# A recurrent attention kernel on one core: working tiles share fewer buffers, a turned operand is kept in DRAM, and more of a streamed weight stays in SBUF

## The chip, the cores and the metric

The kernel runs on one core of a Trainium2 chip. The metric is the device time of one launch in microseconds. Before the change three runs took 2093.66, 2095.27 and 2100.72 us, median 2095.27. One further execution, taken with the hardware profiler, gave the page and the trace that are read below.

## The reference, cut to what matters

```python
x  = A_x                                   # [1, 2048, 1024] bf16
xn = layernorm(x)
out = x + A(xn, mem0, Wq, Wk, Wv, Wo) + B(xn, w_r, w_gate, w_up, w_down)

def A(x, mem0, ...):                       # 32 heads of 128, segments of 32 rows, M = 8 memory rows
    mem = mem0
    for s in range(64):
        h = concat(mem, x[32*s : 32*s+32])              # 40 rows
        q, k, v = h @ Wq, h @ Wk, h @ Wv                # 1024 x 4096 each
        p = softmax(mask(q @ k.T * 128**-0.5))          # memory rows see all; others causal
        o = (p @ v) @ Wo                                # 4096 x 1024
        mem = o[:8]                                     # recurrence
        outs.append(o[8:])

def B(x, ...):                             # router r = x @ w_r picks 2 of the 2048 rows; they alone get
    ...                                    # silu(x@w_gate) * (x@w_up) @ w_down * sigmoid(r), added to x
```

So 64 steps follow one another, each with only 40 rows against four weight matrices of 8 MB, and the memory rows of a step need the end of the step before.

## The kernel before, in words

**Rows.** The 8 memory rows and the first 24 rows of a segment make up the 32 "main" rows of a step (XM = 24, XL = 8). The last 8 rows of a segment, the "left" rows, don't depend on the recurrence until attention. They are gathered for four segments at a time: a group G is four steps, j = s % 4, and its 32 left rows go through Q, K, V as one operand STL in the steps before they are needed. `left_of(s)` says which matrix's left pass a step carries: V of its own group in j=0, Q of the next group in j=1, K of the next group in j=2, nothing in j=3.

**Weights.** The four matrices are cut into 64 granules of 128 x 2048 bf16 (512 KB): 48 for Q, K and V in six phases p0 to p5 of eight (`PHASES`: Q half 0, K half 0, Q half 1, K half 1, V half 0, V half 1), then 16 for Wo (w = 0 to 15, two heads each). 43 granules stay in SBUF for the whole kernel (`wres`). 21 are streamed again in every step from packed copies in DRAM (`wsc`) through a pool of five 4 KB slots (`g`), in order, by SP's queue; `after(s, g)` issues the load of the next streamed granule when one was used. Three streamed granules are partly kept elsewhere: granule 10 wholly and granule 19 by half in PSUM (KEPT, copied into the slot by ACT and DVE), and of granule 35 (HALF, the V phase) the first 1024 columns in the SBUF tile HB. So a step reads 18 granules of 512 KB and two halves of 256 KB.

**A step.** PE takes the granules in order: four column-tiled matmuls with ST (the turned main rows, L638), and where a left pass is due four more with STL (L621). Work that hangs between granules is hooked by (phase, granule): `hook(2, 6, scores(0))` runs after granule 6 of phase 2. After each of p0 to p3 ACT copies the result to XB (L654), PE turns it at (p+1, 3) and ACT or DVE copies it to QT or KT; after p4 and p5 ACT copies VM (L674), and in j=0 VL (L678). `scores` and `soften` run on PE, DVE and ACT, `attend` at (5,5), (5,7), w=5 and w=8. `add_x` at (5,3) starts WO in a PSUM buffer of the pool psA (two buffers, which PSm shares). The projection L689 takes the 16 Wo granules. Then ACT and DVE copy WO to OB, four POOL DMAs store the rows (L748), PE turns OB, and DVE writes the memory rows into the next ST (L281): the next step starts.

**Left rows.** In j=1 and j=2 the results of the left pass go by ACT to XBl (L659, in the single buffer "bD") and by four POOL DMAs to ql_d in DRAM (L664), at hook (p+1, 5); each step loads its part as LX (L454), which PE turns and ACT copies to QKL at (1,5). The left outputs of a group are accumulated in WL (PSUM, pool psL, one buffer "accl" shared with PSl and OPa): in j=3, streamed granules right behind WO's matmuls, the resident ones partly in `fill` at the step's end and five in the next step. x of the left rows comes in at w=1 by a matmul with IDENT on XL (L725), which `sum_left` has scaled on DVE at (5,6). In the next j=0, at (3,0), ACT copies WL to OL (buffer "vl", which VL uses from the end of p4) and POOL stores it (L762).

**STL.** In j=0 XL of the next group is loaded at (3,0), normed by DVE at (5,6), turned by PE at w=13 and copied by ACT to STL (L304 to L308); the first four left passes of the next step run already as `fill` at the end of j=0.

**The first step** (s=0) loads everything: all weights, x (`load_x`, 4 MB), and DRAM-to-DRAM copies of the streamed granules by POOL (`copy_block`). In it DVE takes the row statistics of the 16 x tiles after granules 1 to 15, and after granules 18 to 33 `router_tile(t)`: L223 writes the normed tile to XR, L225 multiplies it with w_r, sums it and writes its products over XR. The last ten resident granules live in the homes of x tiles, XR and MISC, so they are loaded late.

**Buffers.** The pool "one" has one buffer for each tag: bA, bB, bC, bD, bE of 1 KB, kt, st, stl, otl, vl and a few small ones. A new tile of a tag waits until the readers of the last one are done. PTB, the PSUM tile for all transposes, is a single buffer too. The order on each engine is the order of the program (manual schedule); POOL and SP issue their DMAs in order.

Of the kernel before, what the change touches and what calls it, by code (L numbers as in the profile page):

```python
# [8 lines left out]
BF16 = mybir.dt.bfloat16  # L9
F32 = mybir.dt.float32  # L10
# [18 lines left out]
def kernel(  # L29
# [102 lines left out]
    HB = const.tile([P, 1024], BF16, name="HB")  # L132
# [87 lines left out]

    def router_tile(t):
        XR = home(hx, [P, D], BF16, "XR")
        nc.vector.tensor_scalar(out=XR[:, :], in0=xt(t), scalar1=RI16[:, t, 0:1], scalar2=RI16[:, t, 1:2],  # L223
                                op0=ALU.subtract, op1=ALU.mult)
        nc.vector.tensor_tensor_reduce(out=XR[:, :], in0=XR[:, :], in1=WRB, scale=1.0, scalar=0.0,  # L225
                                       op0=ALU.mult, op1=ALU.add, accum_out=RF[:, t:t + 1])
# [91 lines left out]
    def fetch():  # L318
        if not flow:
            return  # L320
        s, g = flow.pop(0)
        t = wstream.tile([P, 2048], BF16, tag="g", name="g")
        c = columns(g, s)
        if s == 0 and g == HALF:
            nc.sync.dma_start(out=HB[:, :], in_=granule_dram(g)[:, 0:1024])
            nc.sync.dma_start(out=t[:, c], in_=granule_dram(g)[:, c])
        elif s == 0:
            nc.sync.dma_start(out=granule_out(t, g), in_=granule_dram(g))
        elif c is not None:
            nc.sync.dma_start(out=t[:, c], in_=wsc[g][:, :])  # L330
        queued.append((g, t))

    def part(g, t, jq):
        return HB[:, 512 * jq:512 * (jq + 1)] if g == HALF and jq < 2 else t[:, 512 * jq:512 * (jq + 1)]


    def keep(g, t):
        for c, K in KEPT_COLS[g].items():
# [4 lines left out]
            XK = one.tile([P, 512], BF16, tag="kt", name="XK")  # L343
# [145 lines left out]
    for s in range(NSEG):  # L489
# [9 lines left out]
        def transposes(mat, half, XB):  # L499
# [13 lines left out]
        def left_keys(half):  # L513
            nc.vector.tensor_copy(out=KT[half][:, :, 32:NK], in_=qkl[0][:, :, 2 * half + 1, :])  # L514
# [66 lines left out]
        def get_left():  # L581
            nxt["xl"] = load_left(G if j == 3 else G + 1)

        def prep_left():
            if j == 0:
                norm_left(nxt["xl"], G + 1)
            else:
                sum_left(nxt["xl"], G)

# [35 lines left out]
        for p, (mat, half) in enumerate(PHASES):  # L625
# [26 lines left out]
            if mat < 2:  # L652
                XB = one.tile([P, 512], BF16, tag=("bC", "bA")[half], name="XB")
# [3 lines left out]
                def store_ql(mat=mat, half=half, PSl=PSl):  # L657
                    XBl = one.tile([P, 512], BF16, tag="bA" if s == 0 and mat == 1 and half == 0 else "bD", name="XBl")
# [22 lines left out]
        WO = nxt["wo"]  # L681
        if s + 1 < NSEG:
            new_lx(s + 1)

        def project(PS, w, Gv, lhs, last):
            for hs in range(2):
                h = 2 * w + hs
                for g in range(4):
                    nc.tensor.matmul(PS[32 * g:32 * g + 32, 0:256], lhsT=lhs(h),  # L689
                                     rhs=Gv[:, D * hs + 256 * g:D * hs + 256 * (g + 1)], start=False,  # L690
# [15 lines left out]
        behind = []  # L706
        for w in range(16):
            if w == 5:
                attend(1, 0)
            if w == 8:  # L710
                attend(1, 1)
            Gv = granule(48 + w)
            project(WO, w, Gv, lhs_main, w == 15)
            if j == 3:
                if w in home_w:
# [3 lines left out]
                    else:  # L719
                        todo.append(((2, (1, 2, 4, 5, 7)[len(todo)]), fn))  # L720
                else:
                    behind.append((w, Gv))
                if w == 1:
                    WL = psL.tile([P, 512], F32, tag="accl", name="WL")
                    nc.tensor.matmul(WL[:, 0:256], lhsT=IDENT[:, :], rhs=nxt["xl"][:, :], start=True, stop=False,  # L725
                                     skip_group_check=True)
                if w >= 1:
                    for w_, Gv_ in behind:
                        project(WL, w_, Gv_, lhs_left, False)
                    behind = []  # L730
# [25 lines left out]
        if j == 3:  # L756
# [6 lines left out]
            todo.append(((3, 0), store_left))  # L763
# [107 lines left out]
```

## Time and profile before

| what | value |
|---|---|
| median of three timed runs | 2095.27 us |
| profiled execution, its own time | 2080.72 us |
| its span (first to last instruction) | 2079.2 us |
| mean granted TensorE clock | 0.948 |
| PE / weight loads / DVE / ACT / POOL busy | 80% / 43% / 41% / 32% / 29% |
| SP's hardware queue | 687.69 MB, 89.1% of 16 DMA engines' span |
| POOL's software queue | 36.34 MB, 5.5% |
| first step (to the first L281 after it) | ends at 132.2 us |
| 63 further steps | about 29.9 us each, to 1982.5 us |
| the rest (last step and the two expert rows) | to 2079.2 us |

A page gives for each group of instructions its line, engine, operation, the tiles it writes and reads, how many there are, their busy time and mean, and the idle time of that engine just before them with what ended it ("issue" is time in which the engine waited for nothing that the profile shows). [...]

### The profile page before, as it was taken

To read this page: it belongs to the slowest core of one execution; us is meant where nothing else is said; L and a number is where in the kernel's file an instruction comes from. 1 tells how busy PE (TensorE), PEld (TensorE's weight loads), DVE (VectorE), ACT (ScalarE), POOL (GpSimd) and SP (SyncE) were. 2 spreads that over 40 slices of the span, in tenths; PEclk is the share of its full clock that TensorE was granted. 3 is DMA by queue.
4 is the path that set the end of the run, shared out by engine and by line. 5 is a ranking of instruction groups with operands and counts; after the bars stand their busy time and mean duration, and the time that the engine had idled before them with its cause. 6 is when DMAs were issued, how large, how long until landed. Compare 5 with 4: busy or idle time off the path is not lost.

```text
span 2079.2 us, 82974 instructions
## 1 busy us (share of the span) xinstructions
PE 1671.3 (80%) x36024; PEld 893.3 (43%) x36024; DVE 846.3 (41%) x2716; ACT 670.8 (32%) x1867; POOL 597.2 (29%) x1142
## 2 busy tenths in 40 slices
PE   3568888888798888888888888888888788888855
PEld 1224444444354444445444444444444444544433
DVE  5733343444434433443444434433443344344420
ACT  0123333333333233333333333333333333333320
POOL 3313233323333232333323232332323223322120
PEclk8679999999999999999999999999999999999986
DMA  9999999999999899999999999999999999999996
GB/s 365 402 350 370 337 340 346 347 347 354 361 334 375 316 342 340 347 368 331 368 340 362 359 353 360 347 372 344 366 341 346 332 359 353 330 360 350 366 389 261
DMA packets 244925, 729.33 MB, mean 351 GB/s; under 512 B 49616, under 2 KB 55792, under 8 KB 244560
## 3 DMA queue, kind: packets, MB, share of 16 engines
q1 hardware_dynamic: 203584, 687.69, 89.1%
q0 software_dynamic: 40976, 36.34, 5.5%
q8 instruction: 282, 4.62, 0.9%
q14 instruction: 83, 0.68, 0.1%
HBM read 711.09 MB, written 22.55 MB: 353 GB/s over the span
## 4 chain that ended last, share of the span: by engine, by line
DMA 59%; PE 28%; issue 5%; ACT 4%; POOL 2%; DVE 1%; ACTq 0%; SPq 0%; POOLq 0%; DVEq 0%
DMA g<-wsc 45%; PE PSm L638 12%; PE WO L689 5%; PE PSl L621 3%; DMA out_dram<-OL 3%; DMA ql_d<-XBl 3%; PE WL L689 2%; DMA wres<-in_A_Wo_dram 2%; PE BT L502 1%; DMA XP<-in_A_x_dram 1%; POOL out_dram L762 1%; POOL ql_d L664 1%; DMA g<-in_A_Wv_dram 1%; DMA out_dram<-XN 1%; DMA wres<-in_A_Wq_dram 1%
## 5 line engine op out<-in xcount | busy, mean ns | idle before, releaser
L638 PE MATMUL PSm<-wres,ST 128*32 128x512 bf16 x8192 | 705.5, 388 | 7.8 <-DVE ST L281 5.4
L638 PEld LDWEIGHTS <-ST 128*32 128x32 bf16 x12288 | 324.3, 96 | 505.2 <-issue 229.6
L638 PE MATMUL PSm<-g,ST 128*32 128x512 bf16 x3968 | 414.9, 389 | 144.8 <-DMA g<-wsc 125.3
L654 ACT CAST XB<-PSm 128x512 bf16<-128x512 f32 x256 | 150.4, 587 | 413.6 <-PE PSm L638 409.9
L748 POOL DMA_DIRECT2D out_dram<-XN x256 | 131.2, 519 | 505.3 <-DVE XN L746 489.4
L689 PEld LDWEIGHTS <-OT 128*32 128x32 bf16 x8192 | 208.1, 99 | 122.5 <-issue 95.7
L689 PE MATMUL WO<-wres,OT 128*32 128x256 bf16 x5632 | 236.3, 283 | 15.9 <-DMA wres<-in_A_Wo_dram 13.6
L664 POOL DMA_DIRECT2D ql_d<-XBl x256 | 154.2, 609 | 297.6 <-ACT XBl L659 292.0
L621 PE MATMUL PSl<-wres,STL 128*32 128x512 bf16 x2048 | 195.4, 392 | 12.2 <-ACT VL L678 11.4
L689 PE MATMUL WO<-g,OT 128*32 128x256 bf16 x2560 | 135.7, 288 | 69.2 <-DMA g<-wsc 58.6
L251 POOL DMA_DIRECT2D XN<-in_A_x_dram x256 | 130.3, 512 | 126.6 <-PE BT L502 45.2
L454 POOL DMA_DIRECT2D LX<-ql_d x63 | 36.6, 581 | 403.3 <-ACT OT L573 220.5
L511 DVE COPY KT<-BT 128x512 bf16<-128x512 bf16 x128 | 54.4, 425 | 224.0 <-PE BT L502 224.0
L674 ACT CAST VM<-PSm 128x512 bf16<-128x512 f32 x128 | 77.7, 607 | 163.8 <-PE PSm L638 159.4
L350 DVE COPY g<-KEPT 128x512 bf16<-128x512 bf16 x252 | 95.1, 419 | 71.7 <-PE PSm L638 46.4
L502 PE MATMUL BT<-IDENT,XB 128*128 128x128 bf16 x1024 | 102.6, 223 | 24.5 <-ACT XB L654 20.4
L621 PEld LDWEIGHTS <-STL 128*32 128x32 bf16 x3072 | 84.1, 97 | 80.5 <-issue 33.8
L528 DVE TENSOR_TENSOR BS<-BS,MASK 128x320 f32<-128x320 f32 x128 | 64.0, 500 | 130.3 <-PE BS L524 130.3
L573 ACT CAST OT<-BS 128x128 bf16<-128x128 f32 x160 | 42.6, 266 | 216.1 <-PE BT L568 216.1
L502 PEld LDWEIGHTS <-XB 128*128 128x128 bf16 x1024 | 58.9, 98 | 123.5 <-ACT XB L654 75.3
L514 DVE COPY KT<-QKL 128x128 bf16<-128x128 bf16 x128 | 22.3, 175 | 213.7 <-ACT QKL L463 212.8
L621 PE MATMUL PSl<-g,STL 128*32 128x512 bf16 x992 | 104.1, 388 | 5.6 <-ACT XBl L659 5.6
(156 smaller groups left out, 2379.4 us busy)
## 6 DMA issues: line engine op xcount, KB each, us to landing
g<-wsc SPq DMA_DIRECT2D x1134, 512.0 KB, 6.2
g<-wsc SPq DMA_DIRECT2D x126, 256.0 KB, 5.1
ql_d<-XBl POOLq DMA_DIRECT2D x256, 32.0 KB, 5.7
LX<-ql_d POOLq DMA_DIRECT2D x63, 128.0 KB, 5.8
MW<-in_B_w_gate_dram SPq DMA_DIRECT2D x16, 448.0 KB, 9.3
MW<-in_B_w_up_dram SPq DMA_DIRECT2D x16, 448.0 KB, 9.0
wres<-in_A_Wk_dram SPq DMA_DIRECT2D x12, 512.0 KB, 12.9
wres<-in_A_Wo_dram SPq DMA_DIRECT2D x11, 512.0 KB, 15.2
```

The source lines that it names most:

```text
L251: nc.gpsimd.dma_start(out=XN[32 * g:32 * g + XM, :], in_=x2[s * SEG:s * SEG + XM, 256 * g:256 * (g + 1)])
L350: copy(out=t[:, 512 * c:512 * (c + 1)], in_=KEPT_COLS[g][c])
L502: nc.tensor.transpose(out=PTq[:, il, :, :].rearrange("p j r -> p (j r)"), in_=XB[:, il * P:(il + 1) * P], identity=IDENT[:, :])
L511: nc.vector.tensor_copy(out=KT[half][:, :, 0:32], in_=pv)
L528: nc.vector.tensor_tensor(out=S4, in0=S4, in1=MASK[:, :].unsqueeze(1).to_broadcast([P, 4, 2 * NK]), op=ALU.add)
L621: nc.tensor.matmul(PSl[32 * jq:32 * jq + 32, :], lhsT=STL[:, g % KC, :], rhs=part(g, Gv, jq), start=first_, stop=last_, tile_position=(0, ...
L638: nc.tensor.matmul(PSm[32 * jq:32 * jq + 32, :], lhsT=ST[:, kc, :], rhs=part(g, Gv, jq), start=(kc == 0), stop=(kc == KC - 1), tile_positi ...
L654: nc.scalar.copy(out=XB[:, :], in_=PSm[:, :])
L664: nc.gpsimd.dma_start(out=ql_d[left[mat]][:, 32 * jq + c0:32 * jq + c0 + 8, :], in_=XBl[32 * jq:32 * jq + 32, :])
L674: nc.scalar.copy(out=VM[half][:, :], in_=PSm[:, :])
L689: nc.tensor.matmul(PS[32 * g:32 * g + 32, 0:256], lhsT=lhs(h), rhs=Gv[:, D * hs + 256 * g:D * hs + 256 * (g + 1)], start=False, stop=(last ...
L748: nc.gpsimd.dma_start(out=out2[s * SEG:s * SEG + XM, 256 * g:256 * (g + 1)], in_=OB[32 * g:32 * g + XM, :])
```

## The change

Five things change together; lines of the old kernel are in brackets.

- HB holds 1536 instead of 1024 columns of granule 35, so its streamed part is 128 x 512 (128 KB instead of 256 KB in each step).
- The tag bD is gone. XL and the XBl tiles go to bA, bB and bC, XB to "bE" (Q) and "kt" (K), XK to "vl". The stores of the left Q and K move from (p+1, 5) to (p+1, 0), and that of K half 1 in j=2 to w=8 of the projection; for this `attend(0, .)` of j=2 uses the PSUM columns of BS instead of "accl".
- The copy of the left keys into KT goes from DVE to ACT, behind the transposes.
- STL is no longer made in j=0. In the first step each `router_tile` turns the left columns of its normed tile: two times four transposes into PTB, each followed by an ACT copy into a staging tile; every fourth tile POOL writes the staging tile to stl_d in DRAM. In j=0 a single POOL DMA (64 KB) brings STL, issued ahead of LX once the last left pass of V has read the old one.
- WL starts with its first projected granule (w=2). XL is loaded once a group, at w=9 of j=3, `sum_left` runs at (1,5) and the IDENT matmul at (2,3) of the next step, the five carried granules at (1,2) to (2,2), and OL is stored at (2,4).

```diff
     def columns(g, s):
         if g == HALF:
-            return slice(1024, 2048)
+            return slice(1536, 2048)
...
+    stl_d = dram.tile([NT, P, 256], BF16, name="stl_d")
...
-    HB = const.tile([P, 1024], BF16, name="HB")
+    HB = const.tile([P, 1536], BF16, name="HB")
...
     def router_tile(t):
         XR = home(hx, [P, D], BF16, "XR")
         nc.vector.tensor_scalar(out=XR[:, :], in0=xt(t), scalar1=RI16[:, t, 0:1], scalar2=RI16[:, t, 1:2],
                                 op0=ALU.subtract, op1=ALU.mult)
+        if t % 4 == 0:
+            stage[0] = one.tile([P, 4, 8, 4, XL], BF16, tag=("otl", "vl")[t // 4 % 2], name="STG")
+        for c in range(2):
+            for k in range(4):
+                nc.tensor.transpose(out=PTB[:, k * P:(k + 1) * P], in_=XR[:, (4 * c + k) * P:(4 * c + k + 1) * P],
+                                    identity=IDENT[:, :])
+            nc.scalar.copy(out=stage[0][:, t % 4, 4 * c:4 * c + 4, :, :],
+                           in_=PTB.rearrange("p (k s r) -> p k s r", k=4, s=4)[:, :, :, XM:SEG])
+        if t % 4 == 3:
+            nc.gpsimd.dma_start(out=stl_d[t - 3:t + 1].rearrange("t p c -> p t c"),
+                                in_=stage[0].rearrange("p t k s r -> p t (k s r)"))
         nc.vector.tensor_tensor_reduce(out=XR[:, :], in0=XR[:, :], in1=WRB, scale=1.0, scalar=0.0,
                                        op0=ALU.mult, op1=ALU.add, accum_out=RF[:, t:t + 1])
...
     def load_left(G):
-        t = one.tile([P, 256], BF16, tag="bD", name="XL")
+        t = one.tile([P, 256], BF16, tag="bC", name="XL")
...
-            XK = one.tile([P, 512], BF16, tag="kt", name="XK")
+            XK = one.tile([P, 512], BF16, tag="vl", name="XK")
...
-                left_keys(half)
+                nc.scalar.copy(out=KT[half][:, :, 32:NK], in_=qkl[0][:, :, 2 * half + 1, :])
                 nc.vector.tensor_copy(out=KT[half][:, :, 0:32], in_=pv)
...
-                if half == 0 and j > 0:
+                if half == 0 and j in (1, 3):
                     sums[half] = [psL.tile([P, 512], F32, tag="accl", name="OPa")[:, 0:4 * NK], OPS[1]]
...
-        if j == 3 or (j == 0 and G + 1 < NT):
-            hook(*((4, 4) if s == 0 else (2, 0) if j else (3, 0)), get_left)
-            hook(5, 6, prep_left)
...
-                XB = one.tile([P, 512], BF16, tag=("bC", "bA")[half], name="XB")
+                XB = one.tile([P, 512], BF16, tag=("bE", "kt")[mat], name="XB")
...
-                    XBl = one.tile([P, 512], BF16, tag="bA" if s == 0 and mat == 1 and half == 0 else "bD", name="XBl")
+                    home_ = "bC" if mat == half == 0 else "bB" if mat == half == 1 and s > 0 else "bA"
+                    XBl = one.tile([P, 512], BF16, tag=home_, name="XBl")
...
+                elif PSl is not None and mat == half == 1:
+                    nxt["ql"] = store_ql
                 elif PSl is not None:
-                    hooks.setdefault((p + 1, 5), []).append(store_ql)
+                    hooks.setdefault((p + 1, 0), []).append(store_ql)
...
         WO = nxt["wo"]
+        if j == 0 and G + 1 < NT:
+            STL = one.tile([P, KC, SEG], BF16, tag="stl", name="STL")
+            nc.gpsimd.dma_start(out=STL.rearrange("p k r -> p (k r)"), in_=stl_d[G + 1])
...
             if w == 8:
                 attend(1, 1)
+                if "ql" in nxt:
+                    nxt["ql"]()
...
-                        todo.append(((2, (1, 2, 4, 5, 7)[len(todo)]), fn))
+                        todo.append((((1, 2), (1, 4), (1, 7), (2, 1), (2, 2))[len(todo)], fn))
                 else:
-                    behind.append((w, Gv))
-                if w == 1:
-                    WL = psL.tile([P, 512], F32, tag="accl", name="WL")
-                    nc.tensor.matmul(WL[:, 0:256], lhsT=IDENT[:, :], rhs=nxt["xl"][:, :], start=True, stop=False,
-                                     skip_group_check=True)
...
+                    first = WL is None
+                    if first:
+                        WL = psL.tile([P, 512], F32, tag="accl", name="WL")
+                    project(WL, w, Gv, lhs_left, False, first)
+                if w == 9:
+                    group["xl"] = load_left(G)
...
-            if w == 13 and j == 0 and G + 1 < NT:
-                STL = new_stl(nxt["xl"])
...
+            def add_left(WL=WL):
+                nc.tensor.matmul(WL[:, 0:256], lhsT=IDENT[:, :], rhs=group["xl"][:, :], start=False, stop=False,
+                                 skip_group_check=True)
+
+            todo.append(((1, 5), lambda G=G: sum_left(group["xl"], G)))
+            todo.append(((2, 3), add_left))
+            todo.append(((2, 4), store_left))
```

More of the change, by code (lines that the diff above doesn't have):

```diff
@@ L219 @@
     hx = resident[-2]
+    stage = [None]
     def router_tile(t):
@@ L324, in fetch @@
         if s == 0 and g == HALF:
-            nc.sync.dma_start(out=HB[:, :], in_=granule_dram(g)[:, 0:1024])
+            nc.sync.dma_start(out=HB[:, :], in_=granule_dram(g)[:, 0:1536])
             nc.sync.dma_start(out=t[:, c], in_=granule_dram(g)[:, c])
@@ L333, in part @@
     def part(g, t, jq):
-        return HB[:, 512 * jq:512 * (jq + 1)] if g == HALF and jq < 2 else t[:, 512 * jq:512 * (jq + 1)]
+        return HB[:, 512 * jq:512 * (jq + 1)] if g == HALF and jq < 3 else t[:, 512 * jq:512 * (jq + 1)]
     def keep(g, t):
@@ L579, in clear_pl @@
             nc.gpsimd.memset(PL.rearrange("p i a k -> p (i a) k")[:, :, XL * jp:XL * (jp + 1)], 0.0)
[L581 to L588, printed above, removed]
         for at, fn in todo:
@@ L681, with project @@
         WO = nxt["wo"]
+        if j == 0 and G + 1 < NT:
+            STL = one.tile([P, KC, SEG], BF16, tag="stl", name="STL")
+            nc.gpsimd.dma_start(out=STL.rearrange("p k r -> p (k r)"), in_=stl_d[G + 1])
         if s + 1 < NSEG:
             new_lx(s + 1)
-        def project(PS, w, Gv, lhs, last):
+        def project(PS, w, Gv, lhs, last, first=False):
             for hs in range(2):
@@ L689, in project @@
                     nc.tensor.matmul(PS[32 * g:32 * g + 32, 0:256], lhsT=lhs(h),
-                                     rhs=Gv[:, D * hs + 256 * g:D * hs + 256 * (g + 1)], start=False,
+                                     rhs=Gv[:, D * hs + 256 * g:D * hs + 256 * (g + 1)], start=(first and hs == 0),
                                      stop=(last and hs == 1), tile_position=(0, 32 * g), skip_group_check=True)
@@ L705 @@
         final = (carried or late or [None])[-1]
-        behind = []
+        WL = None if j == 3 else group.get("wl")
         for w in range(16):
```

7 lines of the change are left out of this document (removed).

## The prediction

> **What bounds the kernel now.** I read the page's slices first, then the queues and the chain, then the idle time of single instruction groups, and last the stretches of one step with their granted clock and DMA share.
>
> ```profile
> span 2079.2 us, 82974 instructions
> DMA  9999999999999899999999999999999999999996
> q1 hardware_dynamic: 203584, 687.69, 89.1%
> DMA 59%; PE 28%; issue 5%; ACT 4%; POOL 2%; DVE 1%; ACTq 0%; SPq 0%; POOLq 0%; DVEq 0%
> ```
>
> The DMA engines are busy nearly throughout, and the chain that ended last runs over transfers for 59% and over PE for 28%. So the weight stream is the bound, with places in which PE holds it up. To find these I marked each step's start by the ST copy of L281 in the timeline. Steps 4 to 62 take 29.74 us (j=0), 30.08 (j=1), 28.89 (j=2) and 30.70 (j=3); the packets' time fills 94, 98, 98 and 93% of them. The stretches of one j=3 step (starting at 670.37) and of the j=2 step before it say why:
>
> ```profile
> 682.00:690.60 8.60, 6.78 (x149) 3.12 (x149) 4.34 (x14) 2.55 (x10) 0.00 (x0) 1.00 1.02 392
> 690.60:692.90 2.30, 0.20 (x9) 0.06 (x1) 1.91 (x9) 0.76 (x4) 0.57 (x1) 0.79 1.02 406
> 692.90:697.60 4.70, 4.70 (x101) 2.88 (x102) 0.39 (x2) 0.35 (x2) 0.00 (x0) 0.50 0.67 241
> 697.60:702.00 4.40, 4.40 (x124) 3.45 (x124) 0.68 (x3) 1.57 (x6) 0.01 (x1) 0.87 0.68 223
> ...
> 663.80:670.37 6.57, 3.52 (x96) 2.29 (x84) 0.68 (x4) 1.59 (x6) 0.03 (x1) 1.00 1.03 405
> ```
>
> Columns: stretch, its length, busy time of PE, weight loads, DVE, ACT, POOL, then granted clock, DMA share, GB/s. In j=2 (last line) the output projection waits for loads (PE 3.52 of 6.57 us, DMA 1.03). In j=3 PE stands still for 2.3 us, runs at half clock behind that, and the DMA share drops to 0.67, since full slots wait for PE. The instruction is the one at L725:
>
> ```profile
> L725 PE MATMUL WL<-XL,IDENT 128*128 128x256 bf16 x16 | 4.8, 302 | 25.9 <-issue 20.3 <-ACT VM L674 5.6
> PE PSl L621 <- ACT VL L678: 11.4, 11, 3.3
> ACT XBl L659 <- DMA ql_d<-XBl: 57.3, 30, 5.0
> ```
>
> It adds x at w=1 and needs sum_left, which DVE ends at 692.8 in that step. The other two waits are of j=0 (VL waits for OL's store) and of j=1 and 2 (the single buffer bD).
>
> **The change part by part**, for the profiled execution (span 2079.2, 2080.72 with what lies around it).
>
> *The quarter granule.* 128 KB less in each of 63 steps. In the trace's packet records a 2,048-byte packet takes 84 ns and a 1,024-byte one 46 ns (medians); each of 16 engines carries 8 of granule 35's rows, so 8 x 38 ns = 0.30 us a step, 19 us in all. Granule 35 lies in the V phase, where the DMA share is 1.01 to 1.04 in all four kinds of step, so it counts whole; from below I allow 13 (no gain in a third of the steps), from above 63 x 0.55 = 35, half the difference between the landing times of 512 KB (6.2) and 256 KB (5.1). I take 19.
>
> *WL in j=3.* The add moves to (2,3) of the next step, sum_left to (1,5), and the first WL matmul stands at w=2, when ACT's copies of OPa have just ended (690.6 in that step). The stall of 25.9 us in 16 steps goes. What is late next is the stream: a j=3 step without it should idle the DMA as a j=2 step does, 0.69 us in place of 2.02, so 1.33 x 16 = 21 us. Bounds: 0 if the loads take it all, 38 (rival 3). XL is loaded at w=9: four issues at 0.6, landing 5.8, so some 8 us, and (1,5) is about 9 us away; DVE there has nothing urgent before KT at (2,3).
>
> *j=0.* norm_left, two transposes and the STL copy go (0.3 us of PE); OL is stored four granules earlier, so the VL wait (11.4 us in 15 steps) goes. DMA share late in j=0 is about 0.91, so I count half of 11.4 + 15 x 0.3: 8 us less. In their place STL comes by a POOL DMA that waits for the last read of the old one (22.6 us into the step) and is needed 6.0 us later. XL's landing is 4.4 to 7.7, median 5.8: late by 0 to 1.9 us, taken at 0.2, 3 us in 15 steps (0 to 28). Behind it on POOL stand LX (needed some 11 us later) and the output stores. Net -5. By the Trainium skill (DMA: Bandwidth & Descriptors, Anatomy of one DMA) such a transfer costs about 2.0 us plus its bytes at 436 GB/s, an estimate of 2.2 us for STL: never late, a sum 3 us lower. The trace speaks against it: the two loads of this queue nearest in size, XL (16 KB, 4.4 to 7.7) and LX (128 KB, 3.9 to 11.1), take 5.8 us in the median.
>
> *Buffers.* bD's waits go (57.3 us of ACT, of which PE sees the 20.4 us at L502). New: VM of half 0 shares bA with the j=1 store of half 1. Its ACT copy stands behind the exp (13.0 us into the step), four issues at 0.61 end at 16.0, the last lands near 21.3; VM was copied at 18.4, and add_x needs its PSUM buffer at 20.2. So PE stalls about 1.7 us where it stalled 1.3 before. j=1 is the step in which the DMA never idles late (share 1.00 to 1.03), and the loads already issued (50, 53, 56, 4 us) cover it: 0, or 16 x 1.7 = 27 without that cover. XB in "kt" waits for PM's transpose by up to 0.4 us, and its reader comes four granules later: nothing. Left keys move from DVE (175 ns) to ACT (268), parallel to the other KT copy: nothing.
>
> *The first step.* This costs.
>
> ```profile
> 57.70:90.90 33.20, 13.45 (x180) 5.40 (x177) 31.94 (x61) 4.89 (x9) 7.76 (x13) 0.65 1.03 400
> 90.90:132.20 41.30, 19.74 (x340) 9.94 (x340) 11.65 (x30) 6.41 (x23) 9.16 (x16) 0.62 1.03 395
> ...
> 57.75 0.61 PE L471 MATMUL BT<-IDENT,XBl 128*128 128x128 bf16 x4
> 58.40 0.27 ACT L472 COPY QKL<-BT 128x128 bf16<-128x128 bf16 x1 [3.09 <-PE BT L471]
> 58.72 0.59 PE L502 MATMUL BT<-IDENT,XB 128*128 128x128 bf16 x4 [0.35 <-ACT QKL L472]
> ...
> 83.22 0.55 DVE L223 TENSOR_SCALAR XR<-XP,MISC 128x1024 bf16<-128x1024 bf16 x1
> 83.81 1.23 DVE L225 CUSTOM_DVE_ANT_0 XR<-XR,MISC 128x1024 bf16<-128x1024 bf16 x1
> 85.08 0.55 DVE L223 TENSOR_SCALAR XR<-XP,MISC 128x1024 bf16<-128x1024 bf16 x1
> ```
>
> DVE works without a gap from 57.7 to 90.6, 1.86 us a router tile. Now the reduction, which overwrites XR, waits for eight transposes with one PSUM buffer between them: four transposes to ACT's copy 0.65, ACT to the next four 0.32, those 0.63, so 1.6 us a tile at half clock and 1.2 at full (0.45+0.32+0.43); at 1.45, 16 tiles hold PE at granule 34 until 114 instead of 90.9. SP runs at most five streamed granules ahead, so in the 56.5 us to 114 it has only 17 loads of 512 KB (1.31 us each at 400 GB/s: 22), about 10 us in flight, 6 of scratch copies and 3 of small ones: 41 us. The DMA engines idle 15, and writing 1 MB of stl_d adds 2.6 at 400 GB/s. I take +17. Bounds: 0, and 26 (1.6 x 16, all of it late).
>
> *Sum:* -19 -21 -5 +17 = **-28 us**, so 2080.7 becomes 2053. The timed median, 2095.27, stands 14.6 us (0.7%) above the profiled execution; I carry the difference over: **2067 us**. Its own range, with a third off or on each term, is 2054 to 2081.
>
> **The rivals.**
> 1. *The first step hides its transposes.* For: DMA share 1.03 there, a queue with 10 us in flight. Against: SP's reach ends at five slots. -45: 2050.
> 2. *Only the bytes and the first step count*, since a removed PE wait becomes a wait for a load. For: in j=1 and j=2 PE already waits for loads. Against: the DMA share 0.67 in j=3. -19 +17 = -2: 2093.
> 3. *The clock comes back too.* In j=3 PE runs 4.7 us at half clock behind the stall, and the projection lasts 9.1 us in the mean (20.64 to 29.73 into the step). At full clock PE needs j=0's 5.9, less 0.3 for the transposes, plus 1.1 for five WL granules: 6.7. If the loads keep up, j=3 gives 2.4 x 16 = 38 instead of 21: -45, 2050. The Trainium skill (TensorE: Matmul & The Clock Gate, Part 1: The HAM clock gate) says that the clock falls to half after an idle window of about 3.4 us; by that rule no stall, no drop. The trace agrees in kind: 0.50 follows this stall, though that was 2.3 us. Against: granule 62 can't land before its turn.
> 4. *Slower: VM waits in bA.* Place: L677 in j=1, PE behind it at add_x. If the four ql_d writes land 1.2 us later than I reckon and no issued loads cover the stall, that is 2.9 x 16 = 46: -28 +46 = +18, 2113. It decides from 2.1 us a step (34/16). For: landings up to 11 us occur for LX. Against: in j=1 PE waits for loads in the projection, 7.5 us for 5.5 of work.
>
> **How the numbers follow.** Forecast 0.47, rival 1 0.15, rival 2 0.15, rival 3 0.10, rival 4 0.13. 0.3% is 6.3 us, about what a measurement can tell from no change: faster below 2089, slower above 2101.6. Forecast, 1 and 3 lie below (0.72), with 0.04 of rival 2; the rest of rival 2 within (0.11); rival 4 above (0.13). The range leaves out rival 4 and the lower tails of rivals 1 and 3: 2047 to 2098.
>
> **What would show it.** Right: q1 about 8.3 MB smaller; no idle at the WL add; j=3 steps near 29.1 us with DMA share over 0.95 in the projection; reductions of the router 3.3 us apart, and the first step ending near 149 instead of 132. Wrong: a first step under 140 (rival 1); j=3 still over 30 us (rival 2); VM in j=1 later than 22 us into the step with the DMA share below 0.9 behind it (rival 4); idle before the first left pass on STL of over a microsecond.

## The result: 0.75% slower, and the profile after

Twenty timed runs of each kernel: the median is 2094.63 us before and 2108.39 us after, a ratio of 1.0075 with a 95% interval of 1.0051 to 1.0099, so some 16 us slower (1% is 21 us here). The forecast was 2067 us, faster. Single runs of one kernel scatter by about 1% (2084.84 to 2109.02 before); the profiled execution of before stands low among its runs (2080.72), that of after (2107.89) at its median, so the two spans lie 27 us apart where the medians lie 14 apart.

The page of the changed kernel: span, slices, the hardware queue, and the group of VM (its busy time, mean ns and, behind the second bar, ACT's idle time before it).

```profile
span 2106.3 us, 83155 instructions
DMA  9888999999999989999999999999999999999997
GB/s 366 304 288 309 349 329 373 339 351 359 344 358 336 339 318 366 349 336 341 336 353 336 361 347 329 345 342 354 355 360 327 372 349 341 346 349 329 365 372 293
q1 hardware_dynamic: 203584, 679.43, 87.8%
L677 ACT CAST VM<-PSm 128x512 bf16<-128x512 f32 x128 | 77.9, 609 | 134.9 <-DMA ql_d<-XBl 69.9
```

The bytes are gone as meant (687.69 MB before, 8.26 MB less), but the queue's share fell instead of the span. The first slices (52.7 us each) now hold 8s, at 288 to 309 GB/s. And ACT waits 69.9 us before VM for something that didn't stand there before: the landing of the stores to ql_d. The same group on the page of before, where the wait was for PE's results:

```profile
L674 ACT CAST VM<-PSm 128x512 bf16<-128x512 f32 x128 | 77.7, 607 | 163.8 <-PE PSm L638 159.4
```

Steps marked as before, by the ST copy (now L296); step means over steps 4 to 62, worked out from the trace:

| us | before | after | forecast |
|---|---|---|---|
| first step ends | 132.1 | 161.4 | +17 |
| j=0 | 29.74 | 29.72 | -0.6 |
| j=1 | 30.08 | 31.22 | -0.3 |
| j=2 | 28.89 | 29.19 | -0.3 |
| j=3 | 30.70 | 28.96 | -1.6 |
| DMA idle in j=0, 1, 2, 3 | 1.72, 0.47, 0.69, 2.02 | 2.23, 2.00, 0.36, 0.46 | |
| granted clock in j=1, j=3 | 0.990, 0.936 | 0.925, 0.977 | |

(The last column takes the forecast's terms apart by step: the quarter granule 0.30 everywhere, 1.33 more in j=3, 5/15 more in j=0. Between the first step's end and 1982.5 us lie 62 steps before, not 63: the last step belongs to the rest.)

**j=3 did what was forecast, and more.** The add of the left x, L768, and the projection of one j=3 step, starting at 1303.27, in stretches like those shown of before (columns as there: stretch, length, busy time of PE, weight loads, DVE, ACT, POOL, clock, DMA share, GB/s; a DMA share is the packets' time as a share of 16 engines' time, and in the rows of this case it reaches 1.04):

```profile
L768 PE MATMUL WL<-XL,IDENT 128*128 128x256 bf16 x16 | 4.4, 273 | 0.0
```

```profile
1314.90:1323.50 8.60, 6.99 (x154) 3.17 (x157) 5.09 (x16) 3.08 (x10) 0.00 (x0) 1.00 0.99 357
1323.50:1328.00 4.50, 4.30 (x145) 3.25 (x138) 2.21 (x11) 1.77 (x9) 1.23 (x3) 1.00 1.01 398
1328.00:1332.00 4.00, 3.00 (x87) 2.37 (x90) 0.29 (x2) 1.23 (x4) 1.76 (x4) 1.00 1.03 404
```

PE no longer idles before the add (25.9 us in 16 steps before), the clock stays at 1.00 where it was 0.50, and the DMA share at 1.01 to 1.03 where it was 0.67.

**j=1 took it back.** The waits of the changed kernel (engine and line, what it waited for, total us, times, longest):

```profile
ACT VM L677 <- DMA ql_d<-XBl: 69.9, 15, 6.1
PE WO L611 <- ACT VM L677: 47.8, 15, 5.0
PE BS L578 <- DVE PL L556: 15.3, 15, 1.5
```

VM waits 4.7 us in each of the 15 j=1 steps with a left pass for the stores out of bA, and PE stands 3.2 us behind it at add_x, which needs the PSUM buffer that VM's copy frees. The group of add_x over all 64 steps, first before and then after, shows in its last part how PE's idle time there grew:

```profile
L611 PE MATMUL WO<-XS,IDENT 128*128 128x256 bf16 x64 | 18.5, 289 | 2.7 <-ACT VM L674 2.6
L611 PE MATMUL WO<-XS,IDENT 128*128 128x256 bf16 x64 | 18.6, 291 | 47.8 <-ACT VM L677 47.8
```

One such step, starting at 637.37: ACT, POOL and PE in the timeline (start, us, engine, line, and in brackets the idle time before it and its releaser), then its stretches:

```profile
650.22 0.59 ACT L660 CAST XBl<-PSl 128x512 bf16<-128x512 f32 x1
651.10 2.40 POOL L665 DMA_DIRECT2D ql_d<-XBl  x4 [3.89 <-ACT XBl L660]
658.05 0.59 ACT L677 CAST VM<-PSm 128x512 bf16<-128x512 f32 x1 [4.10 <-DMA ql_d<-XBl]
658.53 0.43 ACT L548 ACTIVATE BS<-BS 128x320 f32<-128x320 f32 x1
658.69 0.37 PE L611 MATMUL WO<-XS,IDENT 128*128 128x256 bf16 x1 [2.64 <-ACT VM L677]
```

```profile
637.37:655.40 18.03, 15.74 (x308) 7.43 (x308) 6.66 (x18) 6.31 (x13) 9.06 (x17) 1.00 1.01 356
655.40:659.00 3.60, 0.96 (x17) 0.23 (x9) 0.80 (x3) 0.91 (x2) 0.00 (x0) 0.84 1.03 387
659.00:662.20 3.20, 3.20 (x61) 1.32 (x64) 2.96 (x12) 1.02 (x8) 0.00 (x0) 0.50 0.88 330
662.20:668.78 6.58, 6.48 (x172) 4.34 (x168) 1.16 (x6) 2.64 (x11) 0.63 (x2) 0.81 0.86 278
```

The four stores are issued from 651.1 to 653.5, and VM starts at 658.05. While PE stands, the DMA share is 1.03: the loads already issued do cover the stall itself. The loss comes behind it: PE goes on at half clock, holds the full slots longer, and the share falls to 0.88 and 0.86. It is the picture of the old j=3 step, moved to j=1. The exp of half 1 (L548) stands behind VM on ACT and is late too.

**The first step** grew by 29 us. Its stretches after (before, the share was 1.00 to 1.04 from 57.7 to 132):

```profile
57.70:90.00 32.30, 18.23 (x168) 8.86 (x168) 16.38 (x33) 7.36 (x22) 4.30 (x7) 0.55 0.81 312
90.00:120.00 30.00, 18.05 (x145) 8.38 (x141) 15.51 (x27) 6.19 (x21) 7.33 (x12) 0.56 0.56 181
120.00:140.00 20.00, 11.38 (x198) 5.26 (x194) 8.63 (x15) 4.27 (x15) 7.42 (x13) 0.67 0.94 326
140.00:161.40 21.40, 8.48 (x140) 4.70 (x139) 2.32 (x13) 2.04 (x8) 0.13 (x1) 0.50 1.04 392
```

And two router tiles in its timeline:

```profile
65.43 0.54 DVE L227 TENSOR_SCALAR XR<-XP,MISC 128x1024 bf16<-128x1024 bf16 x1
66.03 0.61 PE L233 MATMUL BT<-IDENT,XR 128*128 128x128 bf16 x4
66.68 0.27 ACT L235 COPY STG<-BT 128x128 bf16<-128x128 bf16 x1 [1.30 <-PE BT L233]
66.99 0.58 PE L233 MATMUL BT<-IDENT,XR 128*128 128x128 bf16 x4 [0.35 <-ACT STG L235]
67.62 1.23 DVE L240 CUSTOM_DVE_ANT_0 XR<-XR,MISC 128x1024 bf16<-128x1024 bf16 x1 [1.65 <-PE BT L233]
68.89 0.55 DVE L227 TENSOR_SCALAR XR<-XP,MISC 128x1024 bf16<-128x1024 bf16 x1
```

From one normed tile to the next (65.43 to 68.89) it is 3.46 us, in a chain over DVE, PE, ACT, PE and DVE again; the 16 tiles take until 119.6 instead of 90.6. The DMA engines idle 0.19 x 32.3 + 0.44 x 30 + 0.06 x 20 = 20.5 us, and the packets up to the step's end take 140.7 us per engine instead of 133.2.

### The profile page after: what moved, and what is told of

Its sections match the earlier page's. It is cut to its first block, busy times and chain, and to the rows that moved or that the text cites. A ratio compares the mean times of both kernels' runs of the same rounds, so it can differ in the third digit from the quotient of the medians.

```text
span 2106.3 us, 83155 instructions
## 1 busy us (share of the span) xinstructions
PE 1696.3 (81%) x36122; PEld 901.1 (43%) x36122; DVE 823.5 (39%) x2543; ACT 708.8 (34%) x2012; POOL 573.3 (27%) x1101
## 5 line engine op out<-in xcount | busy, mean ns | idle before, releaser
L638 PE MATMUL PSm<-g,ST 128*32 128x512 bf16 x3904 | 421.3, 395 | 151.2 <-DMA g<-wsc 135.5
L695 PE MATMUL WO<-wres,OT 128*32 128x256 bf16 x5632 | 245.2, 290 | 24.7 <-DMA wres<-in_A_Wo_dram 14.1
L621 PE MATMUL PSl<-wres,STL 128*32 128x512 bf16 x2048 | 195.3, 393 | 1.6 <-issue 0.3
L266 POOL DMA_DIRECT2D XN<-in_A_x_dram x256 | 129.5, 511 | 140.4 <-PE PSm L638 46.4
L677 ACT CAST VM<-PSm 128x512 bf16<-128x512 f32 x128 | 77.9, 609 | 134.9 <-DMA ql_d<-XBl 69.9
L585 ACT CAST OT<-BS 128x128 bf16<-128x128 f32 x192 | 50.9, 265 | 205.7 <-PE BT L580 205.7
L621 PEld LDWEIGHTS <-STL 128*32 128x32 bf16 x3072 | 83.3, 98 | 59.7 <-issue 16.1
L578 PEld LDWEIGHTS <-VM 32*128 32x128 bf16 x2048 | 68.9, 93 | 90.7 <-issue 83.3
L621 PE MATMUL PSl<-g,STL 128*32 128x512 bf16 x976 | 104.9, 396 | 0.0
```

The source lines that it names most:

```text
L266: nc.gpsimd.dma_start(out=XN[32 * g:32 * g + XM, :], in_=x2[s * SEG:s * SEG + XM, 256 * g:256 * (g + 1)])
L578: nc.tensor.matmul(o, lhsT=VM[half][q0:q0 + 32, il * P:(il + 1) * P], rhs=PTm[q0:q0 + 32, il, 0:NK], start=True, stop=False, tile_position ...
L621: nc.tensor.matmul(PSl[32 * jq:32 * jq + 32, :], lhsT=STL[:, g % KC, :], rhs=part(g, Gv, jq), start=first_, stop=last_, tile_position=(0, ...
L638: nc.tensor.matmul(PSm[32 * jq:32 * jq + 32, :], lhsT=ST[:, kc, :], rhs=part(g, Gv, jq), start=(kc == 0), stop=(kc == KC - 1), tile_positi ...
L677: nc.scalar.copy(out=VM[half][:, :], in_=PSm[:, :])
```

## The experiments

Each kernel was timed in turn with the kernel before on the same chip. There were three groups of runs, each on a chip of its own: hb1024, hb1024_bd, wl_only and first_light; early, early_shift, both_1536 and both_1024; both_512, first_dec, j2_back and j2_back_early. The median of before moved between them (2099, 2102 and 2089 us), so the ratios are what is compared. A comparison between groups, or with the changed kernel, takes it that a ratio doesn't depend on the chip; no run tested that. The step means are of one profiled execution each, and the same kind of step can differ by 0.4 us and more between executions.

| run | ratio to before (95%) | first step | j=0 | j=1 | j=2 | j=3 |
|---|---|---|---|---|---|---|
| after | 1.0075 (1.0051 to 1.0099) | 161.4 | 29.72 | 31.22 | 29.19 | 28.96 |
| hb1024 | 1.0078 (1.0051 to 1.0104) | 162.7 | 30.73 | 31.24 | 28.82 | 29.23 |
| hb1024_bd | 0.9905 (0.9876 to 0.9935) | 162.4 | 29.96 | 29.48 | 28.05 | 28.86 |
| wl_only | 0.9861 (0.9807 to 0.9914) | 133.5 | 29.89 | 30.21 | 28.91 | 29.25 |
| first_light | 0.9971 (0.9942 to 0.9999) | 140.4 | 29.81 | 31.72 | 29.21 | 28.76 |
| early | 0.9948 (0.9919 to 0.9978) | 161.7 | 29.94 | 30.63 | 28.78 | 29.28 |
| early_shift | 0.9897 (0.9850 to 0.9945) | 161.1 | 30.12 | 30.26 | 28.79 | 29.46 |
| both_1536 | 0.9806 (0.9762 to 0.9850) | 138.7 | 29.77 | 29.70 | 29.12 | 28.75 |
| both_1024 | 0.9772 (0.9731 to 0.9813) | 139.8 | 29.73 | 29.79 | 28.66 | 29.44 |
| both_512 | 0.9879 (0.9844 to 0.9913) | 138.1 | 29.37 | 30.15 | 28.72 | 29.16 |
| first_dec | 1.0037 (1.0009 to 1.0064) | 147.9 | 29.66 | 31.27 | 29.04 | 29.04 |
| j2_back | 0.9778 (0.9746 to 0.9811) | 138.3 | 29.58 | 29.59 | 28.88 | 29.12 |
| j2_back_early | 0.9763 (0.9731 to 0.9794) | 139.8 | 29.57 | 29.38 | 28.45 | 28.96 |

### hb1024: the quarter granule taken back

```diff
-            return slice(1536, 2048)
+            return slice(1024, 2048)
...
-    HB = const.tile([P, 1536], BF16, name="HB")
+    HB = const.tile([P, 1024], BF16, name="HB")
```

> The changed kernel with HB back at 1024 columns, so 256 KB of granule 35 are streamed again in each step; nothing else. By the forecast's term every kind of step grows by 0.30 us against the changed kernel's 29.72, 31.22, 29.19 and 28.96 (j=0 to 3): +19 us, span about 2125. Rival: j=0 is bound by PE (busy 26.8 of 29.7 us) and j=1 by the wait of VM, so only j=2 and j=3 grow, 0.3 x 31 = +9 us. If bytes don't count at all: within 3 us.

Measured: no difference to the changed kernel that can be told (1.0078 and 1.0075). j=0 grew by 1.0 us in the profile and j=2 shrank by 0.4, both beyond what the bytes can do, so the step means can't settle this small a term. The profiled execution was also the slowest of its 12 (2119.70 us, median 2111.07). And the packets themselves scatter: over steps 4 to 59 the mean 4,096-byte packet of SP's queue took 174.2 to 178.0 ns in nine of the profiles. At 144 such packets per engine and step that is up to 0.55 us a step, more than the 0.30 of the term. The 19 us of the forecast aren't there in this kernel.

### hb1024_bd: the stored tile in a buffer of its own

```diff
-                    home_ = "bC" if mat == half == 0 else "bB" if mat == half == 1 and s > 0 else "bA"
+                    home_ = "bC" if mat == half == 0 else "bB" if mat == half == 1 and s > 0 else "bD" if mat == 0 and s > 0 else "bA"
```

(on top of hb1024, whose free 1 KB it uses)

> As hb1024, and the stored tile of Q half 1 in j=1 gets a 1 KB buffer of its own in place of bA. If VM's wait in bA is what lengthens j=1 (rival 4's mechanism): VM of half 0 about 18.5 us into the j=1 step instead of 21.3, no PE idle at add_x (3.15 us in each j=1 step of the changed kernel), and j=1 shorter by 1.1 us than in hb1024, 18 us in all. If the loads already issued cover that stall, as the forecast took it: VM earlier, but j=1 within 0.3 us of hb1024's.

Measured in the same group of runs as hb1024: 2111 to 2075 us, 1.7% or 36 us, more than the 18 expected. VM's waits for the stores, and the stretches of the j=1 step that starts at 632.36:

```profile
ACT VM L677 <- DMA ql_d<-XBl: 3.3, 2, 2.0
```

```profile
632.36:650.39 18.03, 15.50 (x304) 7.25 (x301) 6.26 (x17) 6.43 (x14) 9.06 (x17) 1.00 0.95 338
650.39:653.99 3.60, 2.75 (x53) 1.08 (x50) 2.98 (x9) 1.51 (x6) 0.00 (x0) 1.00 1.03 402
653.99:657.19 3.20, 3.04 (x106) 2.28 (x105) 1.75 (x9) 1.46 (x7) 0.60 (x1) 1.00 1.03 405
657.19:662.18 4.99, 3.52 (x89) 2.33 (x91) 0.68 (x3) 1.58 (x6) 0.03 (x1) 1.00 1.02 395
```

The wait falls from 69.9 to 3.3 us, PE doesn't stand, the clock stays at 1.00 and the DMA share at 1.02 to 1.03 to the end of the step. In the mean of 14 steps VM starts 17.6 us into the step, not 21.3, and add_x 18.6, not 21.9; j=1 is 1.76 us shorter than in hb1024, and the DMA engines idle 0.11 us in it instead of 1.97. So the shared buffer is what lengthens j=1, and the cover that the forecast relied on doesn't hold. j=1 explains 1.76 x 16 = 28 of the 36. The rest can't be placed: j=0 and j=2 are 0.8 us shorter too, but the profile of hb1024 is of the slowest of its runs and that of hb1024_bd of the fastest (2063.84), so that the spans lie 56 us apart where the medians lie 36 apart. The j=1 steps show the same once more in first_light and both_1024, which differ by this buffer and the 512 columns: 31.72 and 29.79.

### wl_only: the WL part alone, on the kernel before

```diff
-            hook(*((4, 4) if s == 0 else (2, 0) if j else (3, 0)), get_left)
-            hook(5, 6, prep_left)
+            if j == 0:
+                hook(*((4, 4) if s == 0 else (3, 0)), get_left)
+                hook(5, 6, prep_left)
...
+                if w == 9:
+                    group["xl"] = load_left(G)
...
+            todo.append(((1, 5), lambda G=G: sum_left(group["xl"], G)))
+            todo.append(((2, 3), add_left))
+            todo.append(((2, 4), store_left))
```

> The kernel before with the WL part alone: the IDENT add of the left x, sum_left and the carried granules move as in the change; STL, HB and all buffers stay as before. Theory: j=3 falls from 30.70 to about 29.0 us, the clock in j=3 rises from 0.934 to about 0.98, j=0 stays near 29.7: 16 x 1.7 = 27 us less than before. By the forecast's own size 21 us less. Rival (a removed PE wait becomes a wait for a load): j=3 at 30.4 or more, less than 6 us.

Measured: 0.9861, 29 us less than before (by the interval 18 to 40). j=3 falls from 30.70 to 29.25 and its clock rises to 0.969; the other steps stay within 0.15 us. The rival, that a removed PE wait only becomes a wait for a load, falls.

### first_light and first_dec: the router tile of the first step

first_dec writes the products to the other half of XR's home, so the reduction needn't wait for PE; first_light also puts a selection of the left columns in place of the transposes:

```diff
-        XR = home(hx, [P, D], BF16, "XR")
+        XR = home(hx, [P, 2 * D], BF16, "XR")
...
-        nc.vector.tensor_tensor_reduce(out=XR[:, :], in0=XR[:, :], in1=WRB, scale=1.0, scalar=0.0,
+        nc.vector.tensor_tensor_reduce(out=XR[:, D:2 * D], in0=XR[:, 0:D], in1=WRB, scale=1.0, scalar=0.0,
```

```diff
-        for c in range(2):
-            for k in range(4):
-                nc.tensor.transpose(out=PTB[:, k * P:(k + 1) * P], in_=XR[:, (4 * c + k) * P:(4 * c + k + 1) * P],
-                                    identity=IDENT[:, :])
-            nc.scalar.copy(out=stage[0][:, t % 4, 4 * c:4 * c + 4, :, :],
-                           in_=PTB.rearrange("p (k s r) -> p k s r", k=4, s=4)[:, :, :, XM:SEG])
+        for k in range(8):
+            nc.tensor.matmul(BT[:, 32 * k:32 * (k + 1)], lhsT=XR[:, k * P:(k + 1) * P],
+                             rhs=SELL[:, 0, :, :].rearrange("p s r -> p (s r)"),
+                             start=(k == 0), stop=True, skip_group_check=True)
+        nc.scalar.copy(out=stage[0][:, t % 4, :, :, :].rearrange("p k s r -> p (k s r)"), in_=BT[:, 0:256])
```

> The changed kernel with a lighter router tile in the first step: eight matmuls with a 128 x 32 selection in place of two times four transposes, one ACT copy in place of two, and the reduction writes its products to another half of the buffer, so that it doesn't wait for PE. Theory (the chain normed tile, four transposes, copy, four transposes, reduction sets the pace of the first step, and SP's reach of five slots leaves the DMA idle): a tile takes 2.2 us instead of 3.46, PE passes granule 34 near 98 instead of 119, the first step ends near 140 instead of 161, the rest unchanged: 20 us less than the changed kernel. Rival (the bytes set the end: 51.8 MB and the 1 MB written to stl_d): it still ends after 155.

> The changed kernel with the reduction's products in the other half of the buffer, all transposes and copies kept. Theory (a chain over DVE, PE and ACT sets the pace): without the reduction in the chain a tile takes 2.8 us (1.25 for PE's two sets of matmuls, 1.55 for its transposes and ACT's copy) instead of 3.46, PE passes granule 34 near 108, the first step ends near 151. Rival (the transposes' own time on PE sets it, not the chain): 3.4 us a tile and 160, as in the changed kernel.

Measured: the period of a tile falls from 3.46 to 2.45 (first_dec) and 1.92 us (first_light; before 1.85), the first step ends at 147.9 and 140.4. In time first_light is 1.0%, 22 us, below the changed kernel, first_dec 0.4%. So the chain with the reduction in it set the pace. By the ends of the first step, 13.5 us of 21, the transposes themselves were the smaller part; the times, taken in two groups, give the reduction only 8 us of 22 and don't settle the split. The stretches of first_light show that the DMA idle is gone:

```profile
57.70:90.00 32.30, 18.81 (x244) 7.42 (x236) 26.65 (x57) 8.56 (x20) 6.71 (x11) 0.51 1.03 403
90.00:120.00 30.00, 16.64 (x270) 7.59 (x274) 16.57 (x32) 6.73 (x21) 12.24 (x21) 0.71 0.97 329
120.00:140.40 20.40, 8.32 (x140) 4.58 (x132) 1.06 (x5) 1.98 (x8) 0.08 (x1) 0.50 1.01 383
```

What is left against before, some 8 us, is mainly packet time (140.1 us per engine up to the step's end instead of 133.2), in which the 1 MB for stl_d lies.

### early and early_shift: the stores sooner, their dependants later

```diff
-                    hooks.setdefault((p + 1, 0), []).append(store_ql)
+                    hooks.setdefault((p + 1, 0), []).insert(0, store_ql)
...
-        hook(5, 3, add_x)
+        hook(5, 5 if j == 1 else 3, add_x)
...
-        hook(5, 5, lambda: attend(0, 0))
+        hook(5, 6 if j in (1, 2) else 5, lambda: attend(0, 0))
```

(the first pair is early, all three are early_shift; both keep bA shared)

> The changed kernel with ACT's copy to the stored tile placed ahead of what else is hooked at (p+1, 0), so in j=1 ahead of the exp. Theory (VM waits for the landing of the last of four stores in bA): the copy comes 1.1 us earlier (11.7 us into the j=1 step in place of 12.8), VM at 20.2 in place of 21.3, PE idle at add_x 2.0 in place of 3.15 us, j=1 some 0.7 us shorter: 11 us less than the changed kernel. Rival (the wait is for something else on ACT or POOL): VM stays near 21.3 and j=1 near 31.2.

> As early, and what needs VM and PSm's buffer comes later in PE's order: add_x of j=1 at (5,5) in place of (5,3), the first attend of half 0 at (5,6) in place of (5,5) in j=1 and j=2. Theory: PE goes on with the granules of p5 while the stores land, so its idle at add_x and attend in j=1 falls from 3.2 to under 1 us, and in j=2 the wait for DVE in BS from 0.95 to about 0.5: j=1 near 29.8 and j=2 near 28.9, 27 us less than the changed kernel. Rival (the weight stream needs the time anyway): j=1 stays above 30.8.

| mean of 14 j=1 steps (s = 5 to 57), us into the step | after | early | early_shift | hb1024_bd |
|---|---|---|---|---|
| ACT copy to the stored tile | 12.8 | 11.7 | 11.3 | 12.7 |
| last store issued | 15.5 | 15.1 | 14.5 | 15.6 |
| VM starts | 21.3 | 20.7 | 20.2 | 17.6 |
| PE idle at add_x | 3.15 | 1.92 | 1.09 | none over 0.05 |
| granted clock in j=1 | 0.919 | 0.936 | 0.951 | 0.990 |
| length of j=1 (15 steps, as above) | 31.22 | 30.63 | 30.26 | 29.48 |

The idle at add_x, the clock and the length fall together. In time early is 1.3% below the changed kernel, more than the 11 us expected, and early_shift 1.8%, 37 us, with an interval wide enough for the expected 27. The j=1 steps of early explain only 0.59 x 16 = 9 of its 26 us; where the rest comes from stays open. VM moved by only 0.5 us in early, not 1.1: the four issues, 0.6 us each as before, stood further apart in some steps, so the last one came just 0.5 us sooner. early_shift's 30.26 missed the expected 29.8, since VM at 20.2 is still late for add_x; in j=2 the wait for DVE in BS fell from 0.92 to 0.59 us, about as expected.

### both_1536, both_1024, both_512: the parts together, and what 1 KB is worth

both_1536 is early_shift with first_light's router tile; both_1024 is hb1024_bd with it; both_512 is both_1536 with `slice(512, 2048)` and HB at 512.

> early_shift and first_light together, with the 1536 columns kept. Theory: the two add up, first step near 140 and j=1 near 29.8: 2108 - 17 - 27 = 2064 in the timed median, faster than before by 1.5%.

> hb1024_bd and first_light together: 1024 columns kept, the stored tile in a buffer of its own, a lighter router tile. Theory: 2075 - 17 = 2058. Beside both_1536 it tells what the 1 KB is worth as a quarter granule and as a fifth buffer: by the forecast's 0.30 us a step the quarter granule would give 19 us; if j=0 and the first steps can't use it, 10 or less, and both kernels lie within 10 us of each other.

> both_1536 with HB at 512 columns: 256 KB more of granule 35 streamed in each step, twice the change's quarter, with nothing else to hold j=1 up. By the forecast's term 2 x 0.30 us in each of 63 steps: 38 us above both_1536's 2056.6. If j=0, bound by PE, doesn't feel bytes: 28. By the 3 us that hb1024 and the changed kernel lie apart: 6.

Measured: both_1536 is 1.9% below before (1.5 expected) and 2.7% below the changed kernel, and the two parts alone make 1.0 + 1.8, so they add up. The 256 KB more of both_512 cost 0.74%, 15 us, by ratios from two groups, about 8 for a quarter granule (by the two intervals 2 to 13), less than half of the forecast's 19; the step means are too coarse to say which steps use the bytes. both_1024 and both_1536 can't be told apart: as a fifth working buffer the 1 KB gives about as much as with a quarter granule, without any move in PE's order.

### j2_back and j2_back_early: the part of j=2 undone

```diff
-                    home_ = "bC" if mat == half == 0 else "bB" if mat == half == 1 and s > 0 else "bD" if mat == 0 and s > 0 else "bA"
+                    home_ = "bC" if mat == half == 0 else "bD" if half == 1 and s > 0 else "bA"
...
-                elif PSl is not None and mat == half == 1:
-                    nxt["ql"] = store_ql
...
-                if half == 0 and j in (1, 3):
+                if half == 0 and j > 0:
```

(on both_1024; j2_back_early adds the first pair of lines of early)

> both_1024 with the part of j=2 undone: the stored tiles of half 1 share the fifth buffer, K half 1 is stored at (4, 0) again, and attend of half 0 uses the columns of accl in j=2 instead of BS. Theory (an edit that the forecast didn't price: in BS attend waits for DVE's softmax of half 1, 0.94 us of PE in each j=2 step): that idle goes, j=2 from 28.66 to about 28.1, up to 15 us less. Rival (in j=2 PE waits for loads right behind, so the stall is hidden): PE's idle moves to the projection, j=2 within 0.2 us, both kernels within 4 us.

> j2_back with the copies of the stored tiles ahead of the exp, as in early. Candidate for the fastest: with a buffer of its own nothing waits for the stores, so the earlier copy should be worth under 3 us.

Measured: PE's idle before attend, 0.94 us a j=2 step, goes, but its idle for loads in the projection rises from 0.35 to 2.02, and the time is that of both_1024 (0.9778 and 0.9772). So this stall was hidden. The earlier stores add 0.15%, less than can be told. j2_back_early is the fastest kernel run: 2.4% below before (0.9731 to 0.9794), and 3.1% below the changed kernel by the two ratios.

## Why the prediction was wrong, step by step

**Where it failed: the buffers.** The step that failed reads: "the loads already issued ... cover it: 0, or 16 x 1.7 = 27 without that cover". The landing was right: "the last lands near 21.3", and VM started at 21.3. Three things were wrong behind it.
- The stall was 3.15 us, not 1.7. The larger part of the difference is a wrong reading: the forecast has add_x at 20.2 us into the j=1 step, but in the trace of before it starts at 19.4 in the mean of the 14 steps (19.2 with the last j=1 step, which has no left pass). One of them, starting at 611.61, has VM's copy at 18.8 and add_x at 19.5:

```profile
630.41 0.59 ACT L674 CAST VM<-PSm 128x512 bf16<-128x512 f32 x1 [1.79 <-PE PSm L638]
631.11 0.28 PE L611 MATMUL WO<-XS,IDENT 128*128 128x256 bf16 x1
```

With 19.4 the forecast's own sum gives a stall of 2.5 us, and 16 x 2.5 = 40 us without cover. The other 0.6 us came with the change: PE reaches add_x at 18.8 in the changed kernel and 18.6 in hb1024_bd, most likely because the wait for bD ahead of it is gone, so the same landing finds it earlier.
- A stall has a tail. Behind it the clock was 0.50 and 0.81 in the step shown; PE's 9.8 us there hold 3.2 x 0.50 + 6.58 x 0.19 = 2.9 us lost to the clock. The forecast told this of the old j=3 stall (rival 3) and didn't apply it to the new one.
- The cover that was argued from DMA shares of 1.00 to 1.03 did hold during the stall (1.03), but not behind it (0.88 and 0.86): loads already issued cover the time in which they run, and the slots then stay full while PE catches up.

Measured by hb1024 against hb1024_bd it costs 36 us. This is rival 4, at its place (L677, then add_x), above its deciding point of 2.1 us a step and near its price (46) and its time: 2113 told, 2108 measured. It had a chance of 0.13. But it didn't come about as rival 4 has it. The stores landed at 21.2 in the mean, no later than reckoned; it was PE that came earlier than the forecast had it. So one of its signs failed (VM at 21.3, not later than 22) and one held (a DMA share below 0.9 behind it). That 2113 lies so near is partly luck: the first step cost 12 us more than told and the quarter granule gave some 18 less in this kernel, while j=3 gave 8 more, the shared buffer cost 10 less than rival 4's price, and the rest came to -19 (below) where -5 was told for j=0.

**The first step** was right in kind and too small: +17 told, +29 measured. The period was told as 3.3 and is 3.46 in the median; but PE came to granule 34 only near 119, not 114, since four periods were 4.3 to 7.1 us long: the first step's own work stands between the tiles. In the longest (77.15 to 84.26) DVE's reduction ends at 80.5, DVE waits 1.8 us for ACT's exp and makes the softmax of half 0 until 84.3, and PE waits 3.5 us for the next normed tile; before, where PE needed nothing of XR, that period (3.64) held up DVE alone. DMA idle: 15 told, 20.5 measured. Packets: 2.6 told, 7.5 measured, and the larger part of that is not the 1 MB. Rival 1 (hidden) falls.

**j=3** was right in its mechanism and sized low: 21 told, 29 measured (18 to 40), between the forecast and rival 3's 38. The clock did come back.

**The quarter granule** was over-sized: 19 told; about 8 by both_512, nothing that can be told by hb1024. The packet times behind it are confirmed (1,024-byte packets 46 ns, 2,048-byte ones 84), so what fails is "it counts whole". Which steps can't use the bytes stays open; that j=0 is one, with PE busy for 26.8 of 29.7 us, is argued, not shown. It fits that the DMA idle in j=0 rose from 1.72 to 2.23 us with the change while the step kept its length.

**j=0**: 5 us told, none measured in the step mean. The VL wait did go (PE idle at L621 from 0.84 to 0.08 us a step) and STL came in time: its load landed in 5.3 us in the median (4.7 to 11.1), near the 5.8 that the forecast took, and over the whole kernel PE's weight loads waited 0.2 us for it at L621 and 3.2 at L281 ahead of that. PE's idle in j=0 is 2.97 us a step as before: the time came back mainly as waits for loads and small ones in the projection.

**Not priced at all**: attend of j=2 in BS (0.95 us of PE a step). It was luck that it is hidden, as j2_back showed.

**Sums that don't come out.** A third off or on each of the terms 19, 21, 5 and 17 makes 21 us when they are added, so the forecast's own range would be 2046 to 2088, not 2054 to 2081. With landings up to 7.7 us and 6.0 us to go, STL could be late by 1.7 us, not 1.9. Neither reaches the 2108 measured.

The account closes roughly: WL -29, first step +29, the shared bA +36, the quarter granule -1 in this kernel. Against the measured +16 that leaves -19 for the rest of the buffer changes and STL, a remainder that no run measured by itself, and that is itself uncertain by some 15 us, since the measured terms are (WL by 11, the buffer by 8); that bD's waits (PE idle of 1.36 us a j=1 step at the transposes before, 0.44 in hb1024_bd) are part of it is likely.

## What to carry to other kernels

A buffer whose last reader is a DMA store comes free when the store has landed, not when it was issued: count the issues, the landing, and who stands behind the next writer, and take that one's time from the schedule as it will be once the other waits are gone. Price a PE stall with the half clock behind it, and don't set it to nothing because the DMA is busy while it lasts; look at the share in the microseconds behind it. A kilobyte can be worth more as a buffer that ends a wait than as bytes not streamed.

## What the hardware showed

- *The clock.* PE's idle at add_x in j=1 and the granted clock of the 3 us behind it, over the 15 steps of the changed kernel and the ones of early and early_shift that had such an idle: after idles of 2.5 to 5.0 us the clock was 0.50 to 0.74, after idles up to 1.44 us 1.00 in seven of nine cases and 0.50 and 0.72 in the others, and in between anything from 0.50 to 1.00. The Trainium skill (TensorE: Matmul & The Clock Gate, Part 1: The HAM clock gate) gives about 3.4 us as the idle window and calls it free-running. The spread agrees with free-running; that drops follow idles well under 3.4 us does not agree with a plain threshold.
- *Landings.* The 128 KB loads of granule 35 landed in 5.9 us in the median, the 256 KB loads in 4.5; here the size doesn't order them. The 32 KB stores of this case took 5.6 us.
- *Packets.* Up to the first step's end the mean 4,096-byte packet took 173.8 ns instead of 165.7. The DMA engines' idle time is not the reason: in first_light they idled 0.3 us up to that point, and it was 172.0. Why stays open.
